# Two gated linear-attention branches on one core: another order of the q features, M and the output weights by ten spans of four heads

## The chip, the cores and the metric

The kernel runs on one core of a Trainium2 chip. The metric is the device time of one execution in microseconds (us). The core has a matrix engine (PE, with its weight loads shown as PEld), a vector engine (DVE), a scalar engine (ACT), a general engine (POOL) and a queue engine (SP) that issues most DMAs here. Each engine runs its own instructions in order, and the engines wait for each other through semaphores.

## The reference

Two branches, A and B, each a linear attention over the same x (2048 rows, D = 640 features, 32 heads of 20), mixed by a gate:

```python
qkv = (x @ wqkv) -> q, k, v           # per head, 20 features each
phi = lambda t: where(t > 0, t + 1, exp(t)) + 1e-6
pq, pk = phi(q), phi(k)
kv  = einsum("bhsd,bhse->bhde", pk, v)
z   = einsum("bhsd->bhd", pk)
o   = (pq @ kv) / (pq @ z + 1e-6)     # per head
branch = o (heads side by side) @ wo
out = g * A + (1 - g) * B,  g = sigmoid(sum(x * gate_w))
```

## The kernel before, in words

The program is written as a list of operations in one global order, with the tiles that each reads and writes. A small scheduler (`_Sched`) derives the semaphore waits from that; each engine then runs its own operations in the order of the list. Nothing is reordered later, so the order of the list is the order on every engine and on every queue. `_interleave` builds a part of the list: a sequence of main steps (`mains`), into which chains of side steps (`_Chain`) are dropped at given positions.

The kernel never computes v. It uses G = x^T pk (640 x 640) and then M = Wv^T G, keeps of M only the blocks where row and column are of the same head, and multiplies these by wo. The result WP (640 q features x 640 output columns) is applied directly to the scaled pq. The stages are:

1. *k* (`k_tile`): x transposed (XT) times Wk, by 128-row tiles; ACT takes exp, DVE clamps and adds; the result is PK. POOL adds up PK over the rows (`z_add`) into ZP.
2. *q of A, G of A* (`q_tile`, `g_piece`): a q tile has 128 of the 640 q features on partitions and 512 rows of x in columns: 5 matmuls of 512 columns (`mms` at L288 records all matmuls), exp on ACT (L525), clamp (L530) and sum (L535) on DVE, into PQ. From its third on, a q tile uses the three PSUM banks 4, 5, 6 in turn, and so needs the bank that the L535 of the third tile before it has read. A G piece is 4 pairs of matmuls of 512 and 128 columns; ACT copies the finished G to GT (L566).
3. *q of B, G of B*, with side chains for A: `z_turn` and `den` (the denominators: 20 matmuls, heads on 32 partitions times four blocks of rows), four `recip` instructions (L653) into RC, `widen` (DMAs that spread a head's reciprocals over the partitions of its q features, into RX, two slots), `scale` (L673, PQ times RX, in place), and `m_part` (M, masked by a multiplication on DVE into MG and MT). Then `wp_tile` for A and `den` for B.
4. *fin*: PQ times WP, 128 rows at a time, for A and B in turn. ACT scales A's by the gate into TA (which lies over the first six row tiles of PK A), DVE adds B's into OSTG (three slots), SP writes the output. `m_part` and `wp_tile` of B come near the beginning of this stage, and three of B's four `scale` steps and its last `widen` between its output tiles.

Feature order before: feature f of q sits on partition u = f // 5 of tile k = f % 5, so four neighbouring partitions belong to one head in all five tiles, and one map of reciprocals (128 partitions, each head on 4) serves all five. `widen` is 4 DMAs of 32 rows of 1 KB per block of 512 rows, `scale` one DVE instruction over all five tiles (128 x 2560).

In `m_part`, M is computed in five pieces: 4 groups of 128 rows of M, and a fifth with the last 32 rows of each group of 160 (eight heads are 160 features). The fifth needs its weights gathered (WVT, copied by POOL at L849) and goes to MT. `wp_tile` then needs two accumulated sets of matmuls for each tile, one on MG and one on MT, each of four matmuls side by side in the four 32-column strips of the array; ACT copies columns 0 to 511 to SBUF and DVE columns 512 to 639 (L744). `load_wo` brings wo into the buffers of the k weights: one DMA for the first 128 rows of each group and four for the tails, for both branches in the k stage.

Of the kernel before, what the change touches and what calls it, by code (L numbers as in the profile page):

```python
# [8 lines left out]
ACT = mybir.ActivationFunctionType  # L9
# [3 lines left out]
D = 640  # L13
# [13 lines left out]
C_MK1 = 0  # L27
C_MK2 = 160
C_ZM = 320
C_W = 352  # L30
# [9 lines left out]
def _build_consts():  # L40
    cd = np.zeros((128, C_W), dtype=np.float32)
    p = np.arange(128)[:, None]
    hl = (np.arange(160)[None, :] % 32) // 4
    cd[:, C_MK1 : C_MK1 + 160] = (p // DH) == hl
    g2 = (np.arange(160)[None, :] % 32) // 8
    hl2 = 6 + (np.arange(160)[None, :] % 8) // 4
    cd[:, C_MK2 : C_MK2 + 160] = ((p // 32) == g2) & (((128 + p % 32) // DH) == hl2)
    cd[:, C_ZM : C_ZM + 32] = (p // 4) == np.arange(32)[None, :]
    return _bf16_bits(cd)
# [150 lines left out]
def bass_gated_mix__linear_attn_block__linear_attn_block__prompt_kernel(  # L200
# [16 lines left out]
    with ExitStack() as es:  # L217
# [15 lines left out]
        WVT = {X: sb("WVT" + X, [128, NC, 128]) for X in BR}  # L233
# [6 lines left out]
        MG = sb("MG", [128, 4, 160])  # L240
        MT = sb("MT", [128, NC, 128])
# [10 lines left out]
        RX = sb("RX", [128, 2, 512])  # L252
# [68 lines left out]
        def load_wo(eng, X):  # L321
            dma(
                eng,
                "wo" + X,
                WK[X][:, 0:4, 0:D],
                wo[X].rearrange("(g r) f -> r g f", g=4)[0:128],
                writes=[("WK", X, c) for c in range(NC)] + [("WO", X, 0)],
            )
            for g in range(4):
                dma(  # L330
                    eng,
                    "wot%s%d" % (X, g),
                    WK[X][32 * g : 32 * g + 32, 4, 0:D],
                    wo[X][160 * g + 128 : 160 * g + 160, :],
                    writes=[("WO", X, 1, g)],
                    reads=[("WK", X, 4)],
                )
# [51 lines left out]
        pool(lambda e: e.memset(MT[:, :, :], 0.0), writes=[("MT",)])  # L389
# [119 lines left out]
        def q_tile(X, b, k):  # L509
            bk = nq[0] if nq[0] < 2 else 4 + (nq[0] - 2) % 3  # L510
            slot = nq[0] % 3
            nq[0] += 1
            cols = slice(512 * b, 512 * b + 512)

            def wq(c):
                return WQ[X][:, c, :].rearrange("p (u k) -> p k u", k=NC)[:, k]

            mms(
                acc(bank(bk, 0, 512), [(wq(c), XT[:, c, cols]) for c in range(NC)]),
                reads=xt_reads(4 * b, 4 * b + 4) + [("WQ", X)],  # L520
                writes=[("PS", bk)],
                name="q%s%d%d" % (X, b, k),
            )
            act(
                lambda e: e.activation(EQ[:, slot, :], bank(bk, 0, 512), ACT.Exp),  # L525
                reads=[("PS", bk)],
                writes=[("EQ", slot)],
            )
            dve(
                lambda e: e.tensor_scalar(EQ[:, slot, :], EQ[:, slot, :], 1.0, EPS, op0=ALU.min, op1=ALU.add),  # L530
                reads=[("EQ", slot)],
                writes=[("EQ", slot)],
            )
            dve(
                lambda e: e.scalar_tensor_tensor(  # L535
                    out=PQ[X][:, k, cols],
                    in0=bank(bk, 0, 512),
                    scalar=0.0,
                    in1=EQ[:, slot, :],
                    op0=ALU.max,  # L540
                    op1=ALU.add,
                ),
                reads=[("PS", bk), ("EQ", slot)],
                writes=[("PQ", X, b, k)],
            )
            if z_adds and nq[0] > 2:
                z_add(*z_adds.pop(0), [("PQ", X, b, k)])


        def g_piece(X, j, q, pp):  # L550
# [13 lines left out]
            if q == 3:  # L564
                act(
                    lambda e: e.activation(  # L566
                        GT[:, j, :].rearrange("p (k u) -> p k u", k=NC),
                        P[:, 0:D].rearrange("p (u k) -> p k u", k=NC),
                        ACT.Copy,
                    ),  # L570
# [15 lines left out]
        def z_turn(X, bk):  # L586
# [5 lines left out]
                        ZP[:, xi, :].rearrange("p (u k) -> p k u", k=NC)[:, k],  # L592
# [15 lines left out]
                    in1=CB[:, C_ZM : C_ZM + 32].unsqueeze(1).to_broadcast([128, NC, 32]),  # L608
# [48 lines left out]
        def widen(X, b):  # L657
            slot = b % 2
            for r in range(4):
                dma(  # L660
                    "SP",
                    "rx%s%d%d" % (X, b, r),
                    RX[r:128:4, slot, :],
                    RC[32 * b : 32 * b + 32, :],
                    reads=[("RC", i) for i in range(4)],
                    writes=[("RX", slot, r)],
                )

        def scale(X, b):
            slot = b % 2  # L670
            v = PQ[X][:, :, 512 * b : 512 * b + 512]
            dve(
                lambda e: e.tensor_tensor(  # L673
                    out=v, in0=v, in1=RX[:, slot, :].unsqueeze(1).to_broadcast([128, NC, 512]), op=ALU.mult
                ),
                reads=[("RX", slot, r) for r in range(4)],
                writes=[("PQ", X, b, k) for k in range(NC)],
# [3 lines left out]
        def m_part(X, cs, bk):  # L681
            steps = []
            for i, c in enumerate(cs):
                o = bank(bk, 160 * i, 160 * i + 160)
                pairs = []
                for j in range(NC):
                    if c < 4:
                        l = WV[X][:, j, 160 * c : 160 * c + 128]
                        r = GT[:, j, :].rearrange("p (k u) -> p k u", k=NC)[:, :, 32 * c : 32 * c + 32]
                    else:  # L690
                        l = WVT[X][:, j, :]
                        r = GT[:, j, :].rearrange("p (k g u) -> p k g u", k=NC, g=4)[:, :, :, 24:32]
                    pairs.append((l, r))
                steps += acc(o, pairs)
            mms(
                steps,
                reads=[("WV", X), ("WVT", X)] + [("GT", j) for j in range(NC)],
                writes=[("PS", bk)],
                name="m%s%d" % (X, cs[0]),
            )  # L700
            low = [c for c in cs if c < 4]
            n = len(low)
            dve(
                lambda e: e.tensor_tensor(
                    out=MG[:, low[0] : low[0] + n, :],
                    in0=bank(bk, 0, 160 * n).rearrange("p (c u) -> p c u", c=n),
                    in1=CB[:, C_MK1 : C_MK1 + 160].unsqueeze(1).to_broadcast([128, n, 160]),
# [3 lines left out]
                writes=[("MG", c) for c in low],  # L711
            )
            if 4 in cs:
                dve(
                    lambda e: e.tensor_tensor(
                        out=MT[:, :, :].rearrange("p k (g u) -> p k g u", g=4)[:, :, :, 24:32],
                        in0=bank(bk, 160 * n, 160 * n + 160).rearrange("p (k g u) -> p k g u", k=NC, g=4),
                        in1=CB[:, C_MK2 : C_MK2 + 160].rearrange("p (k g u) -> p k g u", k=NC, g=4),
                        op=ALU.mult,
                    ),  # L720
                    reads=[("PS", bk), ("CST",)],
                    writes=[("MT",)],
                )

        def wp_tile(X, k, pp):
            P = PP[pp]
            for j, (lo, hi) in enumerate(((0, 512), (512, D))):
                steps = []
                for i in range(2):
                    for g in range(4):  # L730
                        if i == 0:
                            l, r = MG[:, g, 32 * k : 32 * k + 32], WK[X][:, g, lo:hi]
                        else:
                            l, r = MT[:, k, 32 * g : 32 * g + 32], WK[X][:, 4, lo:hi]
                        steps.append((P[32 * g : 32 * g + 32, lo:hi], l, r, i == 0, i == 1, (0, 32 * g)))
                mms(
                    steps,
                    reads=[("MT",), ("WO", X, 0)] + [("WO", X, 1, g) for g in range(4)] + [("MG", c) for c in range(4)],
                    writes=[("PS", 2 * pp + j)],
                    name="wp%s%d" % (X, k),  # L740
                )
                o, p = WP[X][:, k, lo:hi], P[:, lo:hi]
                (dve if j else act)(
                    lambda e, o=o, p=p, j=j: e.tensor_copy(o, p) if j else e.activation(o, p, ACT.Copy),  # L744
                    reads=[("PS", 2 * pp + j)],
# [101 lines left out]
        for X in BR:  # L847
            pool(
                lambda e, X=X: e.tensor_copy(  # L849
                    WVT[X][:, :, :].rearrange("p c (g u) -> p c g u", g=4),  # L850
                    WV[X][:, :, :].rearrange("p c (g u) -> p c g u", g=4)[:, :, :, 128:160],
                ),
                reads=[("WV", X)],
                writes=[("WVT", X)],
            )
        for X in BR:
            load_wo("SP", X)
# [26 lines left out]
        def den_a():  # L884
# [23 lines left out]
            _Chain(nA + 4, [(0, lambda: m_part("A", (0, 1, 2), 2)), (2, lambda: m_part("A", (3, 4), 3))]),  # L908
# [14 lines left out]
        m_part("B", (3, 4), 6)  # L923
        m_part("B", (0, 1, 2), 7)
# [58 lines left out]
```

## Time and profile before

| what | value |
|---|---|
| median of 3 runs | 196.62 us (196.11 to 196.96) |
| profiled execution, its own time | 197.04 us |
| its span in the profile | 195.3 us |
| PE busy | 190.0 us (97%) |
| DVE busy | 131.8 us (67%) |
| ACT busy | 77.1 us (39%) |
| POOL busy | 45.3 us (23%) |
| granted PE clock | 1.0 |
| moved by DMA | 15.14 MB, HBM read 9.27 MB |

All durations in this text are from that one profiled execution. In a row of the timeline the first number is the start in us from the beginning of the span, the second is how long the row's instructions took together, then come the engine, the line of the kernel, the operation, what it writes and reads, the shape and the count; in brackets stands the idle time before it and what ended it. In a row of a group the numbers after the bar are the busy time in us and the mean duration of one in ns. Durations of matmuls overlap, so what a matmul costs is read from start to start.

### The profile page before, as it was taken

How to read it: one execution, taken by the hardware profiler on the slowest of the kernel's cores; microseconds unless marked ns; L12 is line 12 of the kernel's file. 1: busy time of each engine (PE TensorE's matmuls, PEld its weight loads, DVE VectorE, ACT ScalarE, POOL GpSimd, SP SyncE). 2: the span in 40 equal slices, each digit the busy share in tenths (PEclk: the TensorE clock that was granted, in tenths of full speed). 3: DMA queues.
4: the chain of work that ended last, by engine and by line, in shares of the span. 5: the costliest groups of instructions: out<-in, count | busy, mean ns of one | idle time of the engine just before them, and what ended most of it. 6: DMA issues, size and time to landing. Idle time of an engine off the chain costs nothing.

```text
span 195.3 us, 3598 instructions
## 1 busy us (share of the span) xinstructions
PE 190.0 (97%) x1432; PEld 108.4 (55%) x1458; DVE 131.8 (67%) x205; ACT 77.1 (39%) x130; POOL 45.3 (23%) x39
## 2 busy tenths in 40 slices
PE   8999999999999999999999999999999999999994
PEld 4655555555555555555466555555566555555552
DVE  0288899998996787868389799944634455533343
ACT  3266565656633342332322533526124523322311
POOL 2000223244348667566363000000000000000000
DMA  5984569974340000000000111000011032111113
GB/s 184 308 142 92 98 180 371 359 241 134 68 137 0 3 0 0 0 0 3 2 0 3 28 46 34 2 3 3 7 48 31 0 98 69 67 51 53 67 67 101
DMA packets 19907, 15.14 MB, mean 78 GB/s; under 512 B 9393, under 2 KB 19890, under 8 KB 19890
## 3 DMA queue, kind: packets, MB, share of 16 engines
q1 hardware_dynamic: 19170, 14.17, 25.7%
q10 hardware_dynamic: 720, 0.74, 1.1%
q8 instruction: 11, 0.18, 0.4%
q14 instruction: 6, 0.05, 0.1%
HBM read 9.27 MB, written 2.62 MB: 61 GB/s over the span
## 4 chain that ended last, share of the span: by engine, by line
PE 94%; ACT 2%; DMA 1%; issue 1%; DVE 0%; DVEq 0%; ACTq 0%
PE ps L288 93%; DMA XN<-in_A_x_dram 1%; ACT WPB L744 1%; PE ps L411 1%; ACT PKA L778 0%; DVE OSTG L790 0%; DVEq L953 0%; ACTq L152 0%
## 5 line engine op out<-in xcount | busy, mean ns | idle before, releaser
L525 ACT ACTIVATE EQ<-ps 128x512 bf16<-128x512 f32 x40 | 23.9, 597 | 42.6 <-PE ps L288 35.7
L530 DVE TENSOR_SCALAR EQ<-EQ 128x512 bf16<-128x512 bf16 x40 | 24.2, 606 | 13.6 <-ACT EQ L525 13.2
L790 DVE SCALAR_TENSOR_TENSOR OSTG<-ps,SG,PKA 128x640 bf16<-128x640 f32 (+1 forms) x17 | 14.3, 844 | 22.6 <-PE ps L288 21.4
L481 ACT ACTIVATE EK<-ps 128x640 bf16<-128x640 f32 x32 | 22.4, 704 | 16.3 <-PE ps L288 15.5
L288 PE MATMUL ps<-PKA,XN 128*128 128x128 bf16 (+1 forms) x157 | 24.3, 297 | 0.2
L288 PE MATMUL ps<-XT,WQA 128*128 128x512 bf16 x98 | 24.1, 379 | 0.1
L581 POOL TENSOR_TENSOR ZS<-ZS,PKA 128x640 f32<-128x640 f32 x13 | 18.5, 1425 | 23.9 <-DVE PKB L497 12.1
L778 ACT ACTIVATE PKA<-ps,SG 128x640 f32<-128x640 f32 x16 | 12.7, 794 | 28.7 <-PE ps L288 28.7
L288 PE MATMUL ps<-WPA,PQA 128*128 128x128 bf16 (+1 forms) x156 | 23.6, 297 | 0.3 <-ACT WPB L744 0.2
L288 PE MATMUL ps<-WKA,XT 128*128 128x512 bf16 (+1 forms) x156 | 23.4, 303 | 0.2
L288 PE MATMUL ps<-WPB,PQB 128*128 128x128 bf16 (+2 forms) x157 | 23.4, 297 | 0.2
L288 PE MATMUL ps<-PKB,XN 128*128 128x128 bf16 (+1 forms) x155 | 22.8, 296 | 0.5 <-issue 0.3
L288 PE MATMUL ps<-XT,WQB 128*128 128x512 bf16 x98 | 23.1, 379 | 0.1
L288 PE MATMUL ps<-WKB,XT 128*128 128x129 bf16 (+1 forms) x157 | 22.3, 297 | 0.2
L581 POOL TENSOR_TENSOR ZS<-ZS,PKB 128x640 f32<-128x640 f32 x13 | 18.4, 1419 | 12.6 <-DVE PQA L535 7.6
L288 PEld LDWEIGHTS ps<-PKA,XN 128*128 128x128 bf16 x160 | 13.0, 98 | 11.1
L288 PEld LDWEIGHTS ps<-PKB,XN 128*128 128x128 bf16 x160 | 12.6, 98 | 10.7 <-issue 0.4
L288 PEld LDWEIGHTS ps<-WPA,PQA 128*128 128x128 bf16 x160 | 12.9, 98 | 9.7
L288 PEld LDWEIGHTS ps<-WPB,PQB 128*128 128x128 bf16 x160 | 13.0, 98 | 9.2
L288 PEld LDWEIGHTS ps<-WKA,XT 128*128 128x128 bf16 x160 | 12.6, 99 | 9.6 <-DVE XT L425 0.7
L288 PEld LDWEIGHTS ps<-WKB,XT 128*128 128x128 bf16 x160 | 12.4, 97 | 9.6
L492 DVE TENSOR_SCALAR EK<-EK 128x640 bf16<-128x640 bf16 x32 | 14.6, 458 | 2.1 <-ACT EK L481 1.9
(68 smaller groups left out, 168.4 us busy)
## 6 DMA issues: line engine op xcount, KB each, us to landing
out_dram<-OSTG SPq DMA_DIRECT2D x15, 160.0 KB, 1.8
XN<-in_A_x_dram SPq DMA_DIRECT2D x3, 640.0 KB, 8.6
RX<-RC SPq DMA_DIRECT2D x32, 32.0 KB, 1.9
WKB<-in_B_wqkv_dram SPq DMA_DIRECT2D x1, 800.0 KB, 6.8
WQA<-in_A_wqkv_dram SPq DMA_DIRECT2D x1, 800.0 KB, 5.1
WVA<-in_A_wqkv_dram SPq DMA_DIRECT2D x1, 800.0 KB, 10.8
WQB<-in_B_wqkv_dram SPq DMA_DIRECT2D x1, 800.0 KB, 12.0
WVB<-in_B_wqkv_dram SPq DMA_DIRECT2D x1, 800.0 KB, 12.0
```

The source lines that it names most:

```text
L288: ins = pe.matmul(o, l, r, start=st, stop=sp, tile_position=tp)
L411: ins = pe.transpose(dst[:, 128 * i : 128 * i + 128], XN[:, t, 128 * c : 128 * c + 128], IDN[:, :],)
L481: lambda e: e.activation(EK[:, slot, :], P[:, 0:D], ACT.Exp),
L492: lambda e: e.tensor_scalar(EK[:, slot, :], EK[:, slot, :], 1.0, EPS, op0=ALU.min, op1=ALU.add),
L525: lambda e: e.activation(EQ[:, slot, :], bank(bk, 0, 512), ACT.Exp),
L530: lambda e: e.tensor_scalar(EQ[:, slot, :], EQ[:, slot, :], 1.0, EPS, op0=ALU.min, op1=ALU.add),
L581: lambda e: e.tensor_tensor(out=o, in0=a, in1=PK[X][:, t, :], op=ALU.add),
L744: lambda e, o=o, p=p, j=j: e.tensor_copy(o, p) if j else e.activation(o, p, ACT.Copy),
L778: lambda e: e.activation(TA[:, t % 3, :], PP[pp][:, 0:D], ACT.Copy, scale=SG[:, 0, t : t + 1]),
L790: lambda e, lo=lo, hi=hi, at=at: e.scalar_tensor_tensor(out=OSTG[:, slot, lo:hi], in0=PP[pp][:, at : at + hi - lo], scalar=SG[:, 1, t : t ...
```

## The change

The q features get another order. Tiles 0 and 1 share the first 256 features, even ones in tile 0 and odd ones in tile 1; tiles 2 and 3 share the next 256 in the same way; tile 4 has the last 128 in order (`tile_of`). A pair of tiles has the same heads on the same partitions, so there are three maps of reciprocals instead of one, and `widen` becomes 7 DMAs per block of 512 rows (56 instead of 32 in all), whose sources repeat a row of RC over the partitions of its head. RX grows to 2 x 3 x 512 columns. `scale` becomes two DVE instructions, one for tiles 0 to 3 and one for tile 4.

M is cut by its columns into ten spans of 64 q features. The rows that such a span needs are those of the four heads that contain it, 80 rows (`HS` has each span's first head). So `m_part` has 10 x 5 matmuls with 80-wide weights and 64 columns, in place of 5 x 5 with 128-wide weights and 160 columns; the mask is one DVE instruction per part and has no MT part. A tile of WP takes its four strips of 32 features from four spans (or two, for tile 4), and one set of four matmuls is enough. The copy of a WP tile is split in halves of 320 columns, ACT and DVE, and both wait for both banks. The first part of M has 8 spans (40 matmuls), the second 2; B's parts change their order.

wo is loaded as ten blocks of 80 rows, ten DMAs per branch: A's into the k weight buffers of both branches, B's into row tiles 6 to 15 of PK A, after G of A is finished. POOL's copies into WVT and the zeroing of MT go. The table of constants grows from 352 to 800 columns. The GT copy keeps the plain order.

```diff
+NW = 10
+W = 80
+HS = (0, 3, 6, 9, 12, 16, 19, 22, 25, 28)
...
+        def wo_at(X, w):
+            if X == "A":
+                Y = BR[w // NC]
+                return WK[Y][0:W, w % NC, 0:D], ("WK", Y, w % NC)
+            return PK["A"][0:W, 6 + w, :], ("PK", "A", 6 + w)
+
+        def load_wo(eng, X, w):
+            o, key = wo_at(X, w)
+            r0 = DH * HS[w]
+            dma(eng, "wo%s%d" % (X, w), o, wo[X][r0 : r0 + W, :], writes=[("WO", X, w), key])
...
+        def tile_of(row, k):
+            return row[:, 512:D] if k == 4 else row[:, 256 * (k // 2) + k % 2 : 256 * (k // 2) + 256 : 2]
...
-                acc(bank(bk, 0, 512), [(wq(c), XT[:, c, cols]) for c in range(NC)]),
+                acc(bank(bk, 0, 512), [(tile_of(WQ[X][:, c, :], k), XT[:, c, cols]) for c in range(NC)]),
...
-            for r in range(4):
+            runs = (
+                (0, 0, 0, 12, 10), (0, 120, 12, 1, 8),
+                (1, 0, 12, 1, 2), (1, 2, 13, 12, 10), (1, 122, 25, 1, 6),
+                (2, 0, 25, 1, 8), (2, 8, 26, 6, 20),
+            )
+            for n, (i, p0, h0, nh, m) in enumerate(runs):
+                q = 32 * b + h0
                 dma(
                     "SP",
-                    RX[r:128:4, slot, :],
-                    RC[32 * b : 32 * b + 32, :],
+                    RX[p0 : p0 + nh * m, slot, i, :],
+                    RC[q : q + nh, :].unsqueeze(1).to_broadcast([nh, m, 512]),
...
         def scale(X, b):
-            v = PQ[X][:, :, 512 * b : 512 * b + 512]
+            v = PQ[X][:, 0:4, 512 * b : 512 * b + 512].rearrange("p (i a) n -> p i a n", i=2)
             dve(
                 lambda e: e.tensor_tensor(
-                    out=v, in0=v, in1=RX[:, slot, :].unsqueeze(1).to_broadcast([128, NC, 512]), op=ALU.mult
+                    out=v, in0=v, in1=RX[:, slot, 0:2, :].unsqueeze(2).to_broadcast([128, 2, 2, 512]), op=ALU.mult
...
+            v4 = PQ[X][:, 4, 512 * b : 512 * b + 512]
+            dve(
+                lambda e: e.tensor_tensor(out=v4, in0=v4, in1=RX[:, slot, 2, :], op=ALU.mult),
...
-        def m_part(X, cs, bk):
+        def m_part(X, w0, w1, bk):
+            for w in range(w0, w1):
+                ds = slice(DH * HS[w], DH * HS[w] + W)
+                steps += acc(
+                    bank(bk, 64 * (w - w0), 64 * (w - w0) + 64, 0, W),
+                    [(WV[X][:, j, ds], GT[:, j, 64 * w : 64 * w + 64]) for j in range(NC)],
+                )
...
         def wp_tile(X, k, pp):
+            for g in range(4):
+                w = 8 + g // 2 if k == 4 else 4 * (k // 2) + g
+                fs = slice(32 * (g % 2), 32 * (g % 2) + 32) if k == 4 else slice(k % 2, 64, 2)
+                cells.append((w, MG[:, w, fs]))
+            for lo, hi in ((0, 512), (512, D)):
                 mms(
+                        (P[32 * g : 32 * g + 32, lo:hi], l, wo_at(X, w)[0][:, lo:hi], True, True, (0, 32 * g))
+                        for g, (w, l) in enumerate(cells)
...
+            for j, (lo, hi) in enumerate(((0, D // 2), (D // 2, D))):
                 o, p = WP[X][:, k, lo:hi], P[:, lo:hi]
                 (dve if j else act)(
-                    reads=[("PS", 2 * pp + j)],
+                    reads=[("PS", 2 * pp), ("PS", 2 * pp + 1)],
...
-        for X in BR:
-            load_wo("SP", X)
+        for w in range(NW):
+            load_wo("SP", "A", w)
...
-            _Chain(nA + 4, [(0, lambda: m_part("A", (0, 1, 2), 2)), (2, lambda: m_part("A", (3, 4), 3))]),
+            _Chain(nA + 2, [(0, lambda: [load_wo("SP", "B", w) for w in range(NW)])]),
+            _Chain(nA + 4, [(0, lambda: m_part("A", 0, 8, 2)), (2, lambda: m_part("A", 8, NW, 3))]),
...
-        m_part("B", (3, 4), 6)
-        m_part("B", (0, 1, 2), 7)
+        m_part("B", 0, 8, 7)
+        m_part("B", 8, NW, 6)
```

## The prediction

> **What bounds the kernel now.** I read the page's engine totals and its chain first, then the timeline by engine from 93 us on, then the rows of the operations that the change touches.
>
> ```profile
> span 195.3 us, 3598 instructions
> PE 190.0 (97%) x1432; PEld 108.4 (55%) x1458; DVE 131.8 (67%) x205; ACT 77.1 (39%) x130; POOL 45.3 (23%) x39
> PE 94%; ACT 2%; DMA 1%; issue 1%; DVE 0%; DVEq 0%; ACTq 0%
> ```
>
> TensorE (PE) is the chain. Is it busy at its peak? Its timeline says yes:
>
> ```profile
> 88.16 0.34 PE L288 MATMUL ps<-ONE,ZP 128*128 128x32 bf16 x5
> 88.34 1.25 PE L288 MATMUL ps<-XT,WQA 128*128 128x512 bf16 x5
> ...
> 100.48 1.20 PE L288 MATMUL ps<-GT,WVA 128*128 128x160 bf16 x15
> 101.52 1.25 PE L288 MATMUL ps<-PKB,XN 128*128 128x512 bf16 x8
> 102.61 1.24 PE L288 MATMUL ps<-XT,WQB 128*128 128x512 bf16 x5
> ```
>
> Start to start: 5 matmuls of 512 columns take 102.61 to 103.69 where the next piece begins (216 ns each), 4 pairs of 512 and 128 take 101.52 to 102.61 (272 a pair, so 56 for 128), 15 of 160 columns take 1.04 us (69 each), 5 of 32 columns behind 128-wide strided weights take 0.18 us (37 each). So about 0.42 ns a column plus 2.5, with nearly all weight loads hidden. An edit counts only if it changes PE's columns, exposes weight loads, or makes PE wait. VectorE (DVE) can do the last:
>
> ```profile
> 112.69 1.48 DVE L673 TENSOR_TENSOR PQA<-PQA,RX 128x2560 bf16<-128x2560 bf16 x1
> 114.09 0.29 DVE L530 TENSOR_SCALAR EQ<-EQ 128x512 bf16<-128x512 bf16 x1
> 114.42 0.69 DVE L535 SCALAR_TENSOR_TENSOR PQB<-ps,EQ 128x512 bf16<-128x512 f32 x1
> ...
> 123.76 1.48 DVE L673 TENSOR_TENSOR PQA<-PQA,RX 128x2560 bf16<-128x2560 bf16 x1
> ...
> 129.59 0.69 DVE L535 SCALAR_TENSOR_TENSOR PQB<-ps,EQ 128x512 bf16<-128x512 f32 x1
> ```
>
> From 111.8 to 127 DVE has no idle time. Each q tile of B needs the bank that the third tile before it held, freed by the L535 of that one. Counting the L535 rows against the starts of the q matmuls, PE has 1.1 to 2.6 us in hand at tiles 10 to 19; the tightest is tile 19 (starts 127.3; tile 16 freed its bank at 126.2). DVE may become about 1.1 us late before PE waits.
>
> **The change, part by part.**
>
> *WP in one pass.* Each of 5 tiles a branch ran two sets (MG, MT) of four column groups side by side.
>
> ```profile
> 131.72 0.40 PE L288 MATMUL ps<-WKA,MG 128*32 128x512 bf16 x4
> 132.28 0.39 PE L288 MATMUL ps<-WKA,MG 128*32 128x512 bf16 x4
> 132.49 2.67 ACT L744 ACTIVATE WPA<-ps 128x512 bf16<-128x512 f32 x5
> 132.50 0.29 DVE L744 CAST WPA<-ps 128x128 bf16<-128x128 f32 x1 [2.22 <-PE ps L288]
> 134.45 1.25 PE L288 MATMUL ps<-PQB,ZBD 128*32 128x512 bf16 x20
> ```
>
> A tile takes 0.546 us (131.72 to 134.45 is 2.73 for five); one set takes half, 0.272, so at most 1.37 us a branch. But now the copies bind. Each is 320 columns: ScalarE (ACT) costs 597 for 512 and 704 for 640, 0.84 ns a column, so 437; the DVE cast 292 for 128 columns, plus 192 at 1.04 ns (L535's 692 for 512 against L497's 825 for 640), so 492. Three PSUM pairs rotate. In A, ACT first has a GT copy until 132.5, so the first pair comes free at 132.95, tile 4 starts at 133.0, and the den matmuls, which need the third tile's bank, start at 133.75 instead of 134.45: gain 0.70. In B nothing is ahead: from 148.88, the first copies end at 149.86, tile 4 starts at 149.9, tile 5 at 150.3, the next fin at 150.8 instead of 151.7: gain 0.93. Bounds: 0 (all copies in series) to 1.37 a branch. The longer DVE casts lie in idle time (2.22 us before the first).
>
> *M by ten spans.* 25 matmuls of 160 columns (25 x 69 ns = 1.73 us a branch) become 50 of 64 columns behind weights 80 wide. From the columns alone 64 cost 29 ns (1.46 us); no row has 80-wide weights. Bounds: 29, and 98, the weight load's own duration with nothing hidden (4.9 us). The nearest row is the ZP one, 37 ns, where a short matmul also waits on an uncommon weight load; I take 38: 1.90 us, +0.17 a branch, +0.34 in all. The first part grows (15 x 69 = 1.04 to 40 x 38 = 1.52), so q tile 4 comes 0.5 later, but DVE, behind by that much there, drops the MT mask (325 ns) soon after: RC is complete at 108.5 as before. The GpSimd copies (777 and 717 ns) and the zeroing that go were off the path.
>
> The page "TensorE: Matmul & The Clock Gate", sections on LDWEIGHTS and on weight-path perf modes, speaks against this part: loads get fast only with exactly 128 columns, and otherwise take columns / 1.2 ns. Its estimate is 67 ns for 80 columns, or 3.3 us a branch, +3.2 in all; the forecast would become slower by about 2 us. No row here shows an 80-wide load; the 32-wide ones (97 ns) and the 128-wide ones (98) last the same.
>
> *Reciprocals spread in three maps.* 4 DMAs a block become 7, all on SP's queue.
>
> ```profile
> L277 SPq DMA_DIRECT2D RX<-RC x32: 469/592/602, 108.5 to 158.8; - x32
> DMA to landing us min/median/max: 1.7/1.9/3.0
> 2.67 0.43 SPq L277 DMA_DIRECT2D WKA<-in_A_wqkv_dram  x1
> 3.15 0.33 SPq L277 DMA_DIRECT2D GWR<-in_gate_w_dram  x1
> ```
>
> An issue costs 0.59 plus 0.045 between two. The one-row GWR cost 0.10 less than its neighbour, so for the 8, 2, 6 and 8 row ones I take 0.47 to 0.49, and 0.59 for two of the three 120-row ones (0.47 where it follows a small one): 3.9 us a block; bounds 7 x 0.47 = 3.3 and 7 x 0.64 = 4.5. The last DMA (120 rows from 6) lands later than 1.9: 0.8 more taken, 0 to 1. So block 0's second scale starts at about 108.5 + 3.35 + 2.65 = 114.5 and ends at 114.85, where the single scale ended at 114.1. Scale is now two instructions: 2048 and 512 elements at 0.52 ns plus 149 fixed (1482 for 2560), 1.22 and 0.42, which overlap to 1.46 against 1.40. Block by block SP runs 3.9 us against a DVE rhythm of 4.3, so DVE is 0.7, 0.7, 0.8 and 1.2 us late after the four scales of A. Tile 19 has 1.1, and PE itself comes 0.2 later: no stall, just. Queued behind a waiting scale are the EQ and PQ instructions of every later q tile, so any more shows at once. In B the first scale ends at 146.5 (was 145.2), ahead of the M masks, which wait for matmuls until about 147.4. The last widen (t = 0) delays one output DMA by 2 us, with two more staging slots in hand.
>
> *The rest costs nothing on the path.* The 10 loads of wo for B go ahead of A's widen on SP, but wait only for the last g matmuls of A (93.9) and take 10 x 0.47 us, while SP idles until 108.5 (18.9 us of waiting on RC). wo for A is issued from 45 on and used at 131. q weights at stride 2 instead of 5, and GT in plain order: weight loads under 216 ns matmuls are hidden at 118 ns already; the ACT copy took 704 strided, as the plain L481 did.
>
> **Sum.** -0.70 - 0.93 + 0.34 + 0.05 (more waits ahead of WP) = -1.2 us on the profiled 197.04 (span 195.3 plus 1.7 around it). The median of the runs, 196.62, stands 0.4 lower: forecast 195.4.
>
> **Rivals.**
> - *DVE waits for RX and PE with it* (ends slower). With 0.64 for every issue and a landing 1 us later, a block takes 4.5 us, more than DVE's rhythm, and the lateness grows: the four scales end 1.4, 1.6, 2.6 and 3.8 us late. Tile 17 then waits 1.2 for tile 14's bank and tile 19 another 1.15: +2.35, total +1.1, 197.7. It decides from about 4.0 us a block. For it: 0.592 is the median and the rows are many. Against: small transfers were cheaper.
> - *80-wide weight loads are not hidden* (ends slower). At 67 to 70 ns M costs 3.4 us a branch, +3.4 in all: +1.8, 198.4. It loses from 53 ns on. For it: 64 columns last 29 ns, so there is no room. Against: the ZP row.
> - *The copies eat the WP gain.* At 0.5 us a tile in series on DVE nothing is saved and M's +0.3 stays: 196.9. For it: DVE's copy grows from 292 to 492. Against: DVE and ACT are idle there, and three pairs are free.
>
> **How the numbers follow.** Forecast 0.42, stall 0.22, weight loads 0.22, copies 0.14. The forecast's own range is 194.5 to 196.3: M at 29 ns and 0.4 more from WP, or a stall of 0.9. About 0.5% (1.0 us) is what a measurement of this kernel tells from no change. The forecast lies just beyond it: I give 0.31 of its 0.42 to faster, the rest to the same; half of the copies' case and a mild stall go to the same, and some of the copies' case with good weight loads to faster. Faster 0.38, same 0.24, slower 0.38. The range, 194.4 to 199.0, takes in both slow rivals singly and leaves out both at once.
>
> **What would show it.** M: start-to-start of the 80x64 matmuls near 38 ns. WP: den B's first matmul 2.0 us after WP A begins (now 2.73), and fin 1.9 us after WP B begins (now 2.85). Widen: SP's seven issues 3.9 us; PE without a wait on a PQB row between 123 and 129; DVE idle before its scale rows under 2 us each. Wrong if the M matmuls keep 65 ns or more, if a block's issues pass 4.3 us, or if a scale with the repeated operand in the middle runs above 1.3 us.

## The result, and the profile after

The changed kernel takes 219.41 us (median of 4 runs, 217.66 to 219.85) beside 196.64 us for the kernel before (4 runs, 196.11 to 196.96). The ratio is 1.114, interval 1.108 to 1.121: it is slower by 22.8 us. The profiled execution has its own time of 219.35 us and a span of 217.6 us, against 197.04 and 195.3 before.

The page of the changed kernel, its totals, the granted clock in 40 slices and the chain:

```profile
span 217.6 us, 3628 instructions
PE 198.0 (91%) x1428; PEld 105.0 (48%) x1428; DVE 132.6 (61%) x211; ACT 75.5 (35%) x130; POOL 43.4 (20%) x36
PEclk9999999999999999999998599769999699999999
PE 68%; DMA 14%; SPq 8%; DVE 6%; ACT 1%; issue 1%; DVEq 0%; ACTq 0%
```

PE carried 94% of the chain; now it carries 68%, and 22% belongs to transfers and to the queue that issues them (SPq). The clock dips behind PE's waits.

The starts of the stages, before and after, say where the 22.3 us of span went:

| stretch, from start to start | before | after | difference |
|---|---|---|---|
| begin to first q tile of B | 93.78 | 93.37 | -0.4 |
| q of B, to WP of A | 37.94 | 54.86 | **+16.9** |
| WP of A to fin of A, tile 0 | 12.62 | 12.47 | -0.15 |
| fin A0 to WP of B | 4.54 | 7.07 | **+2.5** |
| WP of B to the next fin | 2.83 | 2.66 | -0.2 |
| fin to the end | 43.6 | 47.2 | **+3.6** |

The three large terms in PE's timeline (start, duration, ..., in brackets the wait and what ended it):

```profile
119.87 4.45 PE L292 MATMUL ps<-XT,WQB 128*128 128x512 bf16 x10 [3.67 <-DVE PQB L534]
...
134.67 1.74 PE L292 MATMUL ps<-XT,WQB 128*128 128x512 bf16 x5 [3.85 <-DVE PQB L534]
...
142.12 2.32 PE L292 MATMUL ps<-XT,WQB 128*128 128x512 bf16 x5 [2.35 <-DVE PQB L534]
...
167.77 1.00 PE L292 MATMUL ps<-PKA,MG 80*32 80x512 bf16 x24 [2.27 <-DVE MG L705]
...
191.70 1.53 PE L292 MATMUL ps<-WPB,PQB 128*128 128x512 bf16 x10 [2.27 <-DVE OSTG L781]
```

In the q stage PE waits for L534 (the sum of a q tile, L535 before), which frees its PSUM bank. What holds L534 up stands in DVE's timeline:

```profile
114.39 1.23 DVE L675 TENSOR_TENSOR PQA<-PQA,RX 128x2048 bf16<-128x2048 bf16 x1 [1.85 <-DMA RX<-RC]
118.46 0.42 DVE L683 TENSOR_TENSOR PQA<-PQA,RX 128x512 bf16<-128x512 bf16 x1 [2.85 <-DMA RX<-RC]
...
121.74 1.23 DVE L675 TENSOR_TENSOR PQA<-PQA,RX 128x2048 bf16<-128x2048 bf16 x1
125.99 0.42 DVE L683 TENSOR_TENSOR PQA<-PQA,RX 128x512 bf16<-128x512 bf16 x1 [3.02 <-DMA RX<-RC]
```

L675 and L683 are the two parts of `scale` (tiles 0 to 3, and tile 4). Between them DVE stands still for 2.6 to 3.0 us in each of A's four blocks, until the third map has landed, with the sums of later q tiles behind it in its queue. The first parts start at 114.39, 121.74, 129.14 and 136.93: a block takes 7.4 to 7.8 us, where the scales of the kernel before came every 3.7 us (112.69 to 123.76 for three steps).

The instructions that spread the reciprocals, on SP's queue (duration in ns, minimum / median / maximum):

```profile
L281 SPq DMA_DIRECT2D RX<-RC x56: 583/798/2992, 108.0 to 184.2; - x56
```

By single DMA, the first block's seven issues last 0.96, 0.68, 0.58, 0.85, 0.71, 0.87 and 0.78 us, 5.74 with the gaps. In the next blocks of A the second issue lasts 2.0 to 2.4 us, though it waits for no semaphore, and a block takes 7.4 in the mean. The last DMA (120 partitions from 6 rows) lands 5.45 us after its issue. A DMA reports each DMA engine's landing by itself in the trace, and these reports show on how many engines each of the seven runs: 12, 8, 2, 12, 6, 8 and 6. This is as the Trainium skill has it, "DMA: Bandwidth & Descriptors", section "Why a DMA increments its semaphore by 16 and not by 1": a DMA uses the largest number of engines up to 16 that divides the outermost size (other than 1) of both sides. The same page, in "Rules for kernel authors", warns that an outermost size below 16 confines a DMA to at most that many engines.

M went as forecast:

```profile
100.07 1.69 PE L292 MATMUL ps<-GT,WVA 128*80 128x64 bf16 x40
101.59 1.25 PE L292 MATMUL ps<-PKB,XN 128*128 128x512 bf16 x8
```

40 matmuls in 1.52 us are 38 ns each.

### The profile page after: what moved, and what is told of

Its sections match the earlier page's. It is cut to its first block, busy times and chain, and to the rows that moved or that the text cites. A ratio compares the mean times of both kernels' runs of the same rounds, so it can differ in the third digit from the quotient of the medians.

```text
span 217.6 us, 3628 instructions
## 1 busy us (share of the span) xinstructions
PE 198.0 (91%) x1428; PEld 105.0 (48%) x1428; DVE 132.6 (61%) x211; ACT 75.5 (35%) x130; POOL 43.4 (20%) x36
## 4 chain that ended last, share of the span: by engine, by line
PE 68%; DMA 14%; SPq 8%; DVE 6%; ACT 1%; issue 1%; DVEq 0%; ACTq 0%
PE ps L292 67%; DMA RX<-RC 10%; SPq L281 8%; DMA out_dram<-OSTG 3%; DVE RC L648 2%; DMA XN<-in_A_x_dram 1%; DVE OSTG L781 1%; DVE PQB L534 1%; PE ps L413 1%; DVE EQ L529 1%; DVE PQA L683 1%; ACT PKA L769 0%; ACT GT L565 0%; DVE DT L640 0%; DVE MG L705 0%
## 5 line engine op out<-in xcount | busy, mean ns | idle before, releaser
L292 PE MATMUL ps<-XT,WQB 128*128 128x512 bf16 x100 | 27.8, 425 | 10.2 <-DVE PQB L534 10.2
L529 DVE TENSOR_SCALAR EQ<-EQ 128x512 bf16<-128x512 bf16 x40 | 23.1, 578 | 15.0 <-ACT EQ L524 14.9
L292 PE MATMUL ps<-WPB,PQB 128*128 128x512 bf16 (+2 forms) x160 | 24.0, 299 | 2.3 <-DVE OSTG L781 2.3
L292 PE MATMUL ps<-PKB,XN 128*128 128x512 bf16 (+1 forms) x160 | 25.8, 317 | 0.0
L292 PE MATMUL ps<-WPA,PQA 128*128 128x512 bf16 (+1 forms) x160 | 25.5, 309 | 0.0
L292 PE MATMUL ps<-PKA,XN 128*128 128x512 bf16 (+1 forms) x160 | 24.5, 299 | 0.0
L292 PE MATMUL ps<-WKB,XT 128*128 128x512 bf16 (+1 forms) x160 | 22.5, 299 | 0.0
L292 PEld LDWEIGHTS ps<-XT,WQB 128*128 128x128 bf16 x100 | 9.8, 106 | 23.5 <-DVE PQB L534 12.0
L292 PEld LDWEIGHTS ps<-PKB,XN 128*128 128x128 bf16 x160 | 13.4, 104 | 13.0 <-issue 4.2
```

The source lines that it names most:

```text
L292: ins = pe.matmul(o, l, r, start=st, stop=sp, tile_position=tp)
```

## The experiments

All runs are compared with runs of the kernel before on the same chip (medians 196.58 to 196.75 us). The kernels are edits of the changed kernel; the x and y runs change only the spread (x_rows_alt the copies of WP too), so what they cost is the cost of the spread.

**x_rows: the spread made cheap.** Three DMAs a block, each of 128 different rows.

```diff
-            for n, (i, p0, h0, nh, m) in enumerate(runs):
+            for i in range(3):
...
-                    RX[p0 : p0 + nh * m, slot, i, :],
-                    RC[q : q + nh, :].unsqueeze(1).to_broadcast([nh, m, 512]),
+                    RX[:, slot, i, :],
+                    RC[:, :],
```

> The changed kernel with widen replaced: three DMAs a block, each of 128 plain rows of RC (no row repeated, wrong heads, so the quotients are left out in effect); the same 384 rows a block land. All theories of the slow spread (few engines a transfer, repeated source rows, seven issues) expect the spread to be harmless here: issues of 0.6 us, landing about 2 us, a block in 1.9 us, no PE wait on a PQB row. Then the rest of the change shows by itself: the sum of the prediction, -1.2 us, 195.4 us, ratio 0.994. If the loss has another source (M, WP, the split scale), the time stays above 205.

Measured: 196.34 us, ratio 0.999 (0.998 to 1.000). No wait of PE on a PQB row, q stage 38.04 us, issues of 0.59, landing after 2.1 us. So all of the 22.8 us lie in how the maps are spread; M, WP, the loads of wo and the split `scale` cost nothing, and together gain no more than 0.3.

**x_repeat: repeated rows alone.** Three DMAs, the source 16 rows, each repeated 8 times, on 16 DMA engines.

> As x_rows, three DMAs of 128 rows, but each source row is repeated over 8 partitions (16 rows of RC by 8). Theory of few engines: 16 engines can share 16 rows evenly, so landing stays near 2.3 us and the time near 195.5. Theory of repeated rows: reading one row of SBUF again and again is what is slow; with 8 rows an engine at 0.14 us a row landing passes 3 us and a block takes 3.4 us or more; 196 to 200 us.

Measured: 196.12 us, ratio 0.998 (0.997 to 0.999). The landing takes 3.8 us instead of 2.1, as the theory of repeated rows had it, but without harm to the time. Where six of these DMAs are queued, they land 0.91 us apart (111.79 to 116.33 for five steps): 113 ns for each of an engine's 8 rows.

**x_few: few DMA engines alone.** Three DMAs of 114 different rows (6 engines with 19 rows each).

> As x_rows, three DMAs of plain rows, but 114 rows each, 6 x 19 (the other 14 partitions of RX hold ones and are left out). Theory of few engines: it runs on 6 engines, 19 rows each; three transfers need 57 rows an engine, at 0.07 to 0.14 us that is 4 to 8 us a block; landing over 4 us, PE waits, 200 to 215 us. Theory of repeated rows: nothing is repeated, 0.046 us a row, 195.5 to 196.5 us.

Measured: 196.32 us, ratio 0.999 (0.998 to 1.000). When six DMAs are queued, they land 1.0 us apart (110.97 to 115.97 for five steps): 53 ns a row. Few engines alone do no harm.

**x_seven: the number of issues alone.** The seven DMAs with their partitions, each from different rows.

```diff
-                    RC[q : q + nh, :].unsqueeze(1).to_broadcast([nh, m, 512]),
+                    RC[p0 : p0 + nh * m, :],
```

> The changed kernel with the same seven DMAs a block and the same destinations, but plain source rows instead of repeated ones (120, 8, 2, 120, 6, 8, 120 rows; wrong heads). Theory of the issue cost: seven issues at 0.8 us stay, 5.6 us a block against a rhythm of 4.3 us on DVE, so 203 us or more. Theory of few engines: 120 plain rows go to 15 engines, landing 2.2 us, and with 0.6 an issue 4.0 to 4.3 us a block: 195.5 to 198 us. Theory of repeated rows: the same 195.5 to 198 us.

Measured: 203.82 us, ratio 1.037 (1.034 to 1.040). A block takes 5.6 us to issue, and PE waits 5.2 us in four waits on L534. So the issues alone cost about 7 us of the 22.8.

**y_seven_few and y_seven_rep: seven issues with one more burden.** The first has the large DMAs on 6 engines with different rows, the second repeated rows on 16 engines.

> As x_seven (seven DMAs a block, plain rows, 203.8 us), but each large one has 114 rows, which go to 6 engines, 19 rows each (the missing rows of RX hold ones and are left out). Theory A, few engines by themselves make the spread slow: 61 rows on the busiest engine and a block over 6 us, 210 us or more. Theory B, it takes few engines and repeated rows together: 61 rows at 0.06 us are 3.7 us, under the seven issues (4.8 us at 0.69), so 201 to 205 us, as x_seven.

> The changed kernel with its seven DMAs and repeated rows, but each large one has 112 rows, 16 rows of RC by 7, which all 16 engines share (8 rows of RX each hold ones, wrong heads). Theory C, repeated rows by themselves make it slow: a block over 6 us, 210 us or more. Theory B, both together: 25 rows on the busiest engine at 0.14 us are 3.5 us, under the seven issues (4.5 to 5.6 us), so 200 to 206 us.

Measured: 204.42 us, ratio 1.039 (1.034 to 1.044), and 202.08 us, ratio 1.027 (1.022 to 1.032), at 5.3 and 5.1 us a block. Neither burden adds anything to seven issues, so it is not a sum of three separate causes. One cell was left: both burdens together.

**x_few_rep: few engines and repeated rows, three issues.**

```diff
-                    RC[0:114, :],
+                    RC[32 * b : 32 * b + 6, :].unsqueeze(1).to_broadcast([6, 19, 512]),
```

> Three DMAs a block as in x_few, 114 partitions of each map on 6 DMA engines, but each filled from 6 rows of the reciprocals that are repeated 19 times, as the changed kernel's last DMA of a block does with 20 (the other partitions hold ones and the heads are not the right ones, so the output is not the reference's; all else is the changed kernel). It carries 57 rows a block on its busiest DMA engines where the changed kernel has 44. Theory A (repeated rows on few DMA engines are slow by themselves: about 0.25 us a row there, from the 5.4 us that the 20-row ones took to land): 57 rows need 8 us or more a block, more than VectorE's 4.3, and the time is near or above the changed kernel's 219 in spite of three issues. Theory B (the number of issues is what counts): as x_few and x_repeat, 196.3.

Measured: 238.13 us, ratio 1.213 (1.208 to 1.217), slower than the changed kernel with less than half of its issues. The spread's row and PE's wait on L534 (L538 here) in this run:

```profile
L281 SPq DMA_DIRECT2D RX<-RC x24: 722/3203/3517, 107.9 to 196.2; - x24
PE ps L292 <- DVE PQB L538: 18.1, 4, 6.6
```

The median issue lasts 3.2 us (3.25 with the gap), where the same shape without repetition had 0.69:

```profile
L281 SPq DMA_DIRECT2D RX<-RC x24: 686/690/857, 107.9 to 157.4; - x24
```

That one line is of x_few. With 19 rows for each engine, 3.25 us is 171 ns a row, three times the 53 ns of different rows. This prices all the runs by one rule: a block takes the longer of the sum of its issues and the rows of its busiest DMA engine times the price of a row.

| run | issues a block, us | rows on the busiest engine | times the price | block by the rule | measured effect |
|---|---|---|---|---|---|
| x_rows | 1.9 | 24 | at 53 ns 1.3 | 1.9 | none |
| x_few | 2.2 | 57 | at 53 ns 3.0 | 3.0 | none |
| x_repeat | 2.1 | 24 | at 171 ns at most 4.1 | up to 4.1 | none |
| y_seven_rep | 5.1 | about 25 | at 171 ns at most 4.3 | 5.1 | +5.4 us |
| x_seven | 5.6 | about 28 | at 53 ns 1.5 | 5.6 | +7.2 us |
| y_seven_few | 5.3 | about 61 | at 53 ns 3.2 | 5.3 | +7.7 us |
| the change | 5.7 | 44 | at 171 ns 7.5 | 7.5 (measured 7.4) | +22.8 us |
| x_few_rep | 2.2 | 57 | at 171 ns 9.7 | 9.7 (measured 9.9) | +41.5 us |

The 44 rows are 10 + 1 + 1 + 10 + 1 + 1 + 20 of the seven DMAs, on the engines that take part in all of them. The 171 ns were measured on six engines; for x_repeat and y_seven_rep, on 16, they are taken as an upper bound (x_repeat's own landings give 113). The change's rows lie on 2 to 12 engines, where no run measured a price by itself, so it is in part luck that 7.5 meets 7.4 so closely. Below about 4 us a block nothing is lost, above 5 it is.

**z_fill: is it the clock?** Matmuls of no use fill the waits of PE in the q stage, so that the clock stays up.

```diff
+            _Chain(nA + 17, [(0, lambda: fill(3, 24, 256))]),
+            _Chain(nA + 24, [(0, lambda: fill(3, 30, 256))]),
+            _Chain(nA + 27, [(0, lambda: fill(3, 12, 256))]),
```

> The changed kernel with idle PE time filled: 24, 30 and 12 matmuls of 256 columns on constants into an unused bank ahead of the q tiles that wait 3.7, 3.9 and 2.4 us. If the lower granted clock after a wait costs time by itself: the matmuls after the waits go back from 430 to 216 ns and 1.5 to 3 us come back, 216.5 to 218 us. If the spread's chain on SP and DVE sets every later start, the clock costs nothing: 219 to 219.8 us.

Measured: 221.34 us, ratio 1.125 (1.119 to 1.131). The granted clock rises from 0.81 to 1.00 between 112 and 130 us, and from 0.81 to 0.91 between 130 and 148, yet the last two waits end at 135.07 and 142.60 (134.67 and 142.12 without the filling), and 0.4 us of that was there before the first spread DMA (108.39 instead of 108.01). The slow clock costs nothing there; the arrival of the maps sets the pace.

```profile
135.07 1.25 PE L292 MATMUL ps<-XT,WQB 128*128 128x512 bf16 x5 [0.51 <-DVE PQB L534]
...
142.60 1.25 PE L292 MATMUL ps<-XT,WQB 128*128 128x512 bf16 x5 [2.76 <-DVE PQB L534]
...
192.22 2.85 PE L292 MATMUL ps<-WPB,PQB 128*128 128x512 bf16 x10 [3.71 <-DVE OSTG L781]
```

The time itself met neither expectation: it is 1.9 us above the changed kernel's. The last row says why. The wait for a staging slot in fin, 2.27 us without the filling, became 3.71 and ended at 192.22 (191.70 without it), and this time the clock halved behind it: ten matmuls take 2.64 us from start to start instead of 1.37.

**late_scales: the whole computation, with the spread out of DVE's way.** A's four blocks get a map buffer each, their scales are put where DVE has time, and the outputs go through ScalarE's queue.

```diff
+        def rx(X, b):
+            return (RX[:, 0], RX[:, 1], WQ["A"][:, 0:3, 0:512], EK[:, :, 0:512])[b]
...
-                    (3, lambda: scale("A", 0)),
...
+            _Chain(nA + 19, [(0, lambda: both("A", 0)), (7, lambda: both("A", 1))]),
...
-                    "ACT" if last and i == 0 else "SP",
+                    "SP" if last and i == 1 else "ACT",
```

> The changed kernel, complete, with the same seven slow DMAs a block, but nothing waits for them early: a buffer of its own for each of the four blocks (two in buffers that are dead by then), A's scale steps moved to where their maps have landed (after q tiles 13 and 17, after WP A, after the reciprocals of B), B's as late as fin needs them, output DMAs on ACT's queue. If the spread hurts only through DVE waiting in order in front of the q tiles: 196.3 us, as x_rows (ratio 0.998). If the DMAs also disturb in another way, 198 or more.

Measured: 232.32 us, ratio 1.181 (1.175 to 1.187). In the q stage the theory held: 38.04 us, no wait of PE. But the whole came out far above the 196.3 expected of it, for the rearrangement had two faults of its own. The waits of SP's queue in late_scales (in total, times, longest):

```profile
SPq L281 <- DMA WQA<-RC: 25.7, 12, 4.7
SPq L281 <- DMA EK<-RC: 24.2, 11, 5.1
```

The DMAs of blocks 2 and 3 were recorded as writing the whole buffer, so each one waited for the landing of the one before. And B's reciprocals go into the same buffer RC, which A's last blocks were still being spread from: DVE waited 15.8 us there, and PE 23.7 us for M of B.

**late_fix: without the two faults.** Only the written rows are recorded, B's reciprocals have their own buffer, and A's blocks 2 and 3 and B's block 0 are scaled later.

```diff
-                    writes=[("RX", slot, i, p0)] + {2: [("WQ", "A")], 3: [("EK", j) for j in range(3)]}.get(b, []),
+                    writes=[("RX", slot, i, p0)],
...
+        RCX = {"A": RC, "B": WQ["A"][:, 4, 0:512]}
...
-            both("A", 2)
             den("B", 7)
             for i in range(4):
-                recip(i)
+                recip("B", i)
+            both("A", 2)
+            both("A", 3)
```

> The changed kernel's whole computation, with its seven DMAs a block as they are, but with the spread moved away from VectorE's rhythm: A's four blocks go to four separate map buffers, A's blocks 0 and 1 are scaled at the end of the q stage and 2 and 3 after B's reciprocals, B's block 0 after WP of B; B's reciprocals have a buffer of their own (the run late_scales lacked this), no spread waits for the landing of the one before, and the output DMAs go through ScalarE's queue. Theory (what is slow is only that VectorE waits for the spread's 7.4 us a block, with the q tiles' sums queued behind): no PE wait on a PQB row in the q stage, WP of A at about 131.3, fin of A0 at about 143.7, and a time near that of x_rows, 196.3 (196 to 198: B's block 0 is spread from about 139 and lands at about 151, just when fin of B needs it; up to 1.5 us of wait there). Rival (the transfers themselves slow the core, through the memory or the clock, wherever they lie): still over 205.

Measured: 197.58 us, ratio 1.004 (1.003 to 1.005). The same seven DMAs a block, still about 7.4 us a block, and 21.8 of the 22.8 us are gone. PE's waits in late_fix:

```profile
PE ps L292 <- DVE PQB L691: 1.1, 1, 1.1
PE ps L292 <- DVE WPA L747: 0.8, 1, 0.8
PE ps L292 <- DVE WPB L747: 0.5, 1, 0.5
```

The first is the scale of B's block 0. Its 1.1 us lie in the expected range, but not for the expected reason, a map that lands too late: the last DMA of that block landed at 149.4, and the scale ran without a wait behind VectorE's copies of WP:

```profile
150.85 0.98 DVE L747 CAST WPB<-ps 128x320 bf16<-128x320 f32 x2 [0.24 <-ACT WPB L747]
151.75 1.22 DVE L680 TENSOR_TENSOR PQB<-PQB,RX 128x2048 bf16<-128x2048 bf16 x1
152.88 0.42 DVE L691 TENSOR_TENSOR PQB<-PQB,RX 128x512 bf16<-128x512 bf16 x1
```

So the transfers are not slow for the core as a whole; what cost the time was who waits for them.

**x_rows_alt and late_fix_alt: WP copied by whole tiles.** The other two waits above are the copies of WP. In x_rows and late_fix each engine copies half of a tile, but both halves read both banks of it.

```diff
-            for j, (lo, hi) in enumerate(((0, D // 2), (D // 2, D))):
-                o, p = WP[X][:, k, lo:hi], P[:, lo:hi]
-                (dve if j else act)(
...
+            o, p = WP[X][:, k, :], P[:, 0:D]
+            on_act = k % 2 == (0 if X == "B" else 1)
+            (act if on_act else dve)(
```

> x_rows (three DMAs of plain rows a block, with other heads' reciprocals, so that the spread costs nothing) with the WP copies by whole tiles in turn, as in late_fix_alt. Theory: 0.8 us less than x_rows, about 195.5, with WP A to den of B at 2.2 us and WP B to fin at 1.95. Rival: 196.3 as x_rows.

> As late_fix, and a WP tile is copied whole by one engine, VectorE and ScalarE in turn (in A VectorE first, in B ScalarE first), instead of in halves by both. Theory (the two halves of a tile run one after the other, since both read the same two banks, so that a tile costs about 0.93 us of copying in series): with whole tiles two tiles are copied at once; from the starts of WP A to den of B 2.2 us instead of 2.57, from WP B to fin 1.95 instead of 2.40: 0.8 us less than late_fix, about 195.5 if that has no wait in fin. Rival (the copies are not what sets this, the matmuls are): the same as late_fix within 0.2.

Measured: x_rows_alt 195.77 us, ratio 0.995 (0.994 to 0.996), and late_fix_alt 196.00 us, ratio 0.996 (0.995 to 0.998). WP of A to den of B takes 2.13 us in x_rows_alt instead of 2.57 in x_rows; in B it is 2.15 instead of 2.40 (the record of fin's first matmul is missing in x_rows_alt; its weight load starts at 150.44, and WP of B at 148.30). The 1.95 expected there was not reached: its fourth tile still waits 0.27 us for ScalarE's copy of the first. PE's timeline of late_fix_alt at WP of A and at den of B:

```profile
131.75 0.93 PE L292 MATMUL ps<-WKA,MG 80*32 80x512 bf16 x17
...
133.87 1.26 PE L292 MATMUL ps<-PQB,ZBD 128*32 128x512 bf16 x20
```

late_fix_alt computes all that the kernel must, and is a little faster than both kernels: 0.75 us below the kernel before on the same chip, at the edge of what can be told.

## Why the prediction was wrong, by its steps

It gave 195.4 us (194.4 to 199.0); 219.41 is far outside. Its own sign of being wrong came true: a block's issues passed 4.3 us.

*Reciprocals spread in three maps: this step failed, at its first two terms.* It put a block at 3.9 us, with the small DMAs at 0.47 to 0.49 and the large ones at 0.59, since the one-row GWR load cost less than its neighbour. Measured without anything in the way are 0.58 to 0.87 for the small ones, 0.78 to 0.96 for the large ones, and 5.74 for a block. The prices were taken from a DMA of one row and from one of another shape, and the upper bound of 4.5 from the same rows; no row showed a DMA whose rows are repeated. The second term, a last landing after 2.65 us, was 5.45. It was scaled from the 1.9 us of 32 different rows, without counting how many rows a DMA engine gets. That count with x_few_rep's price gives 7.5 us a block (measured 7.4), which lies outside both bounds.

*DVE 0.7 to 1.2 us late, no stall.* This followed from the 3.9 us, and fell with it. The rhythm of 4.3 us that the block was set against is also only the first of the three intervals between the old scales (4.33, 3.48 and 3.26), so there was less room than it says. The mechanism (q tiles' sums queued behind a waiting scale, PE waiting for the bank) was told rightly, as the first rival: "more than DVE's rhythm, and the lateness grows". Its price of +2.35 us was worked out at 4.5 us a block; at 7.4 the q stage lost 16.9. x_seven, at 5.6, confirms that the loss grows with the block.

*B's first scale ends at 146.5, ahead of the M masks.* It ended at 167.0, and the masks (L705) stood behind it: fin A0 to WP of B grew by 2.5 us.

*The last widen delays one output DMA by 2 us, with slots in hand.* It held DVE for 7.1 us at a staging slot, and PE for 2.27: the output DMA behind it on SP's queue was issued at 185.05 and its slot came free at 190.76, where an output DMA takes 1.8 us to land in the median. The halved clock at the start of this stage, some 1.2 us, is most of the rest of the 3.6, but no cost of its own: z_fill starts the stage at full clock and waits 3.71 at the same place instead of 2.27.

*WP in one pass, -0.70 and -0.93.* Mis-sized: x_rows shows -0.16 (2.73 to 2.57) and -0.43 (2.83 to 2.40). The step let the two 320-column copies of a tile run side by side. They read the same banks, and the scheduler of this kernel orders every two accesses of ScalarE and VectorE to one bank. In x_rows VectorE's first copy starts only when ScalarE's has ended:

```profile
131.79 1.09 ACT L730 ACTIVATE WPA<-ps 128x320 bf16<-128x320 f32 x3
132.25 1.28 DVE L730 CAST WPA<-ps 128x320 bf16<-128x320 f32 x3 [2.68 <-ACT WPA L730]
```

x_rows_alt confirms it: with the copies apart the gain is 0.60 in A and 0.68 in B. The Trainium skill's "PSUM — Partial Sum Buffer", section "PSUM bank collisions raise a hardware error", calls two engines on one bank at once a collision error; no run here tried it. What the prediction called the rival of the copies, 196.9 with no gain from WP, is nearer to x_rows (196.34) than the sum's 195.4.

*M at 38 ns.* Right, but to the digit by luck: the 38 was borrowed from the ZP row, whose weights are 128 wide. By the Trainium skill's "TensorE: Matmul & The Clock Gate", section "LDWEIGHTS (loading the stationary operand)", the estimate for a load of 80 columns was 67 ns. The trace disagrees: each of the matmuls has its own 80-wide load, which lasts 121 ns, and one starts every 38 ns, so the loads overlap one another.

*The rest costs nothing on the path.* Right: x_rows, which holds all of it, has a q stage of 38.04 us against 37.94.

So with a cheap spread the change is worth -0.3 us (x_rows), not the -1.2 of the sum; 0.7 of the difference comes back when the copies are apart (x_rows_alt, -1.0).

## What to carry to other kernels

Price a DMA by two counts, its issue and the rows that fall on its busiest DMA engine, and compare the larger with the rhythm of the engine that waits for it. A transfer that is too slow for that rhythm may cost nothing if what consumes it is moved behind work that must be done anyway, into buffers of its own: here that turned 219.4 us into 197.6 with the same transfers. When two engines share a copy, give them different PSUM banks; on one bank a scheduler like this one makes them take turns.

## What the runs showed of the hardware

- A repeated source row is dear: 171 ns for 1 KB on 6 engines with 19 copies of a row each (x_few_rep), 113 on 16 engines with 8 copies (x_repeat), against 53 for different rows (x_few). Whether the cause is the one source partition that is read again and again was not tried.
- A DMA on fewer engines isn't cheaper to issue. In ns: 590 on 16 engines (x_rows), 803 to 884 on 15 (x_seven, after a first one of 986), 805 to 855 on 12 (the change, after a first one of 962), 663 to 873 on 8 where SP was not held, 690 on 6 (x_few), 583 to 640 on 2.
- When DMA engines are behind, SP itself is held in the issue: 2.0 to 3.0 us in the changed kernel, 3.2 us in x_few_rep, with no semaphore awaited.
- PE's clock halves in stretches of 3.41 us, and what decides, in these traces, is how long PE was busy in the stretch before, not the length of one wait. In the changed kernel the clock was half at 118.24 to 125.06 (two stretches; PE was busy for 0.52 of the first), 135.30 to 138.72, 142.13 to 145.54 and 169.44 to 172.85; in the 3.41 us before each of these PE was busy for a share of 0.40, 0.19, 0.31 and 0.34. The wait of 2.27 us that ended at 167.77 (with one of 0.52 behind it) belongs to the last of them. The wait of the same length that ended at 191.70 left a share of 0.48 in its stretch (189.92 to 193.33), and the clock stayed. In x_seven 0.41 halved it, in z_fill 0.43 did not. "TensorE: Matmul & The Clock Gate" in the Trainium skill, section "HAM oscillation — how this bites in real kernels", names gaps above about 3.4 us; the waits of 2.35 and 2.27 here show that shorter ones can do it.
